# Two attention problems in one kernel: softmax reciprocals moved to GpSimd as powers, and the early loads and phi(K) exps placed anew

## The chip, the cores and the metric

The kernel runs on one core of one Trainium2 chip. The core has TensorE (PE, matrix products), VectorE (DVE), ScalarE (ACT), GpSimd (POOL) and SyncE (SP, which here only issues transfers). Each engine works through its own instructions in their order; semaphores tie them together. The metric is the device time of one execution in microseconds.

## The reference

Two attention blocks are computed side by side, and their outputs are concatenated. Each has sequence length 2048, width 512, 32 heads of 16 (`DH`). Problem B is plain softmax attention. Problem A is "infini-attention" in four segments of 512 tokens: causal softmax inside a segment, plus a read of a memory that the earlier segments filled. All inputs are bf16.

```python
# A, for each segment s of 4
phi = lambda t: jnp.where(t > 0, t + 1.0, jnp.exp(t))
p = _softmax(qs @ ks.T * scale + mask)          # causal inside the segment
a_dot = p @ vs
a_mem = (phi(qs) @ M) / (phi(qs) @ z + 1e-06)
o = g * a_mem + (1.0 - g) * a_dot               # g = sigmoid(beta), per head
M = M + phi(ks).T @ vs ;  z = z + phi(ks).sum()
# B
p = _softmax(q @ k.T * Dh ** (-0.5)) ;  o = p @ v
# both: o @ wo, then concatenate
```

The two divisions matter here: the softmax's by its row sum, and the memory read's by `phi(q) z + 1e-06`.

## The kernel before

**Tiling and order.** Work is cut into units. A unit is one problem, one chunk of 512 queries and one group of 8; a group `hg` holds 4 heads, one in each 32-row band of TensorE's array. There are 32 units of A (4 segments by 8 groups) and 32 of B. Six A units come first, then A and B units are mixed. Two neighbouring groups share a tile `rt` of Q and K (even and odd heads in one 32-row band, told apart by a mask on Q).

For each unit TensorE makes scores into PSUM. Most score blocks get their exp on ScalarE (lines 690, 693, 757). For B, up to 22 blocks of a unit get it on VectorE instead: line 809 turns a 128x512 block into the bits of a rough power of two, line 775 adds two offsets, and three products with scaled copies of V (`VD`, made on GpSimd at line 626) sum to the exp. In A, GpSimd then zeroes the masked part (line 704). TensorE accumulates the product with V into one PSUM bank `acc` (line 915). A column of ones in V gives the row sum as column 16 (`DH`).

**The planner.** Which instruction follows which is decided while the program is built. A loop keeps a clock for each engine (`c["t"]` for TensorE, `c["act"]`, `c["dve"]`, `c["gp"]`), charged by costs in ns (`dve_do`, `act_do`, `gp_do`). It chooses between a score tile, a product with V, and "chores" (projections, memory sums, output projections). A chore has a due time and may have a condition on the clock: `WA_AT` is the earliest planner time at which A's remaining V, K and Q weights may be used, `XB_AT` and `WB_AT` the same for B's transposed inputs and weights. `pick` moves blocks of a B unit from VectorE to ScalarE where the blocks left for VectorE (1050 ns each) would outlast those left for ScalarE (470 ns each). Small filler products with zeros (line 898) keep TensorE busy.

**Start.** Lines 74 to 78 load four tiles of A's X and the first 128 columns of `wk_a` (on ScalarE's queue) and `wq_a` (on SyncE's). TensorE transposes X (line 303), ScalarE and VectorE copy it (line 944), TensorE projects the first Q and K (lines 948, 949), VectorE masks Q (952, 955), and ScalarE copies K (953). The other transfers were issued early on SyncE: `wv_a`, the rest of `wk_a` and `wq_a` (167 to 169), B's transposed X in four parts (173) with B's weights after the first part (176), and the output weights (182, 183). Three memsets of VectorE (92, 93) write one column of each remaining A weight tile first, so that these three transfers wait for them.

**phi(K).** For each K tile of A, `phi_k` issues a transposing transfer on SyncE (line 390). Later, at a planner time 12000 ns past VectorE's clock, ScalarE takes the exp (394) and GpSimd makes min, max and sum (396 to 398). The memory sum `chore_macc` uses it.

**Ends of units.** `finalize` transposes `acc` into `tT` on VectorE (846), takes the reciprocal of column 16 into a slot of `RA` on VectorE (849), and GpSimd multiplies (863 for A's gate, 867 to 870). For the last unit VectorE multiplies. All of `RA` is tested for its range at the end. `chore_am`, the memory read of an A unit, transposes on VectorE (491), adds 1e-6 (494), takes the reciprocal (495), and GpSimd multiplies (498). Of these reads there are 24, of `finalize` 64.

Of the kernel before, what the change touches and what calls it, by code (L numbers as in the profile page):

```python
# [10 lines left out]
ALU = mybir.AluOpType  # L11
AX = mybir.AxisListType
F32 = mybir.dt.float32
F16 = mybir.dt.float16
BF16 = mybir.dt.bfloat16
# [4 lines left out]
P = 128  # L20
H = 32
DH = 16
D = H * DH
# [18 lines left out]
def fast_path(ctx, tc, nc, A_x, A_wq, A_wk, A_wv, A_wo, A_beta, B_x, B_wqkv, B_wo, out, flag):  # L42
# [19 lines left out]
    def wview(w):  # L62
        return w.rearrange("(cc p) n -> p cc n", p=P)
# [21 lines left out]
    n = 1  # L85
# [2 lines left out]
        n *= 2  # L88
    ri = const.tile([P, 32], F32, name="ri")
    nc.vector.transpose(ri[:], ci[:, 0:32])  # L90

    for w in (wv_a[:, 0, 0:1], wk_a[:, 0, P:P + 1], wq_a[:, 0, P:P + 1]):
        nc.vector.memset(w, 0.0)
    rb32 = const.tile([P, 1], F32, name="rb32")
    for j in range(4):
        nc.vector.memset(rb32[32 * j:32 * j + 32, :], 32.0 * j)
# [44 lines left out]
        nc.vector.memset(jm[32 * j:32 * j + 32, j:j + 1], 1.0)  # L141
    mqg = const.tile([P, 4, 2], F32, name="mqg")

    def setup_gates():

        nc.scalar.activation(gcol[:], beta_t[:], ACT.Exp, scale=-1.0)
        nc.vector.tensor_scalar(gcol[:], gcol[:], 1.0, None, ALU.add)
        nc.vector.reciprocal(gcol[:], gcol[:])
        nc.vector.tensor_scalar(omg[:], gcol[:], -1.0, 1.0, ALU.mult, ALU.add)
        g4, m4 = gcol[:].rearrange("p (r t) -> p r t", t=2), mq[:].unsqueeze(1).to_broadcast([P, 4, 2])  # L150
        nc.vector.tensor_tensor(mqg[:], g4, m4, op=ALU.mult)
        for par in range(2):
            to = maskg[:].rearrange("p (r t) j d -> p t r j d", t=2)[:, par]
            j4 = jm[:].unsqueeze(1)
            nc.gpsimd.tensor_tensor(to[:, :, :, DH], j4.to_broadcast([P, 4, 4]), mq[:, par:par + 1].unsqueeze(2).to_broadcast([P, 4, 4]), op=ALU.mult)
            for rt in range(4):
                nc.gpsimd.tensor_tensor(to[:, rt, :, 0:DH], jm[:].unsqueeze(2).to_broadcast([P, 4, DH]),
                                        mqg[:, rt, par:par + 1].unsqueeze(2).to_broadcast([P, 4, DH]), op=ALU.mult)
# [5 lines left out]
    nc.vector.tensor_scalar(sati[:], sat[:], EXP_B, 0.0, ALU.add, ALU.max)  # L164
    nc.vector.tensor_scalar(sat[:], sati[:], 32767.0, None, ALU.is_equal)

    nc.sync.dma_start(out=wv_a[:], in_=wview(A_wv))
    nc.sync.dma_start(out=wk_a[:, :, P:], in_=wview(A_wk)[:, :, P:])
    nc.sync.dma_start(out=wq_a[:, :, P:], in_=wview(A_wq)[:, :, P:])

    xT_b = const.tile([P, 4, S], BF16, name="xT_b")
    def load_xb(q):
        nc.sync.dma_start_transpose(out=xT_b[:, :, q * 512:(q + 1) * 512], in_=xb2[q * 512:(q + 1) * 512, :])
    load_xb(0)
    for w, part in ((wk_b[:], 1), (wq_b[:], 0), (wv_b, 2)):
        nc.sync.dma_start(out=w, in_=wview(B_wqkv)[:, :, part * D:(part + 1) * D])
    for q in range(1, 4):
        load_xb(q)

    WA_AT = dict(v=6000, k=7000, q=8200)  # L180
    XB_AT, WB_AT = (11000, 16000, 19500, 23000), dict(k=12500, q=13000, v=13500)
    nc.sync.dma_start(out=wo_a[:], in_=wview(A_wo))
    nc.sync.dma_start(out=wo_b[:], in_=wview(B_wo))


    E1 = [(9, 0), (10, 1), (11, 2), (13, 0), (14, 1), (15, 2)]
# [80 lines left out]
    def dve_do(ns, ready):  # L267
        c["dve"] = max(c["dve"], ready) + ns
        return c["dve"]
# [12 lines left out]
    def at(time, fn):  # L282
        lcount[0] += 1
        heapq.heappush(later, (time, lcount[0], fn))
# [102 lines left out]
    def phi_k(s, rt):  # L387

        kn = phik_t[(s, rt)] = sb_.tile([P, 4, P], BF16, name="phik", tag="xin", bufs=4)
        nc.sync.dma_start_transpose(out=kn[:], in_=KT_at[(s, rt)][:])  # L390

        def more():
            e = sb_.tile([P, 4, P], BF16, name="ek", tag="e", bufs=2)
            nc.scalar.activation(e[:], kn[:], ACT.Exp)
            act_do(act_cost(512) + 100, c["t"])
            nc.gpsimd.tensor_scalar(e[:], e[:], 1.0, 0.0, ALU.min, ALU.max)
            nc.gpsimd.tensor_scalar(kn[:], kn[:], 3e38, 0.0, ALU.min, ALU.max)
            nc.gpsimd.tensor_tensor(kn[:], kn[:], e[:], op=ALU.add)
            gp_do(1024, c["act"] + LAT)
            gp_do(512, 0, 2.1)  # L400
            phik_at[s] = c["gp"] + LAT
            phik_n[s] = phik_n.get(s, 0) + 1
        at(c["dve"] + 12000, more)

    def chore_k(k, s, rt):
        def evac(bank):
# [77 lines left out]
    def chore_am(u):  # L484
        def fill(bank, _):
            quad(bank, mbds[(u["c"] - 1) % 2][:, u["hg"], :, :].rearrange("p j w -> p (j w)"),
                 PHQ[(u["c"], u["rt"])][0][:], True, True)

        def evac(bank):
            aT = sb_.tile([P, 16, 32], F32, name="aT", tag="aT", bufs=1)  # L490
            nc.vector.transpose(aT[:].rearrange("p c d -> p (c d)"), bank)
            d_done(dve_do(dve_cost(512), c["t"] + LAT))
            r2 = sb_.tile([P, 16, 1], F32, name="r2", tag="r2", bufs=2)
            nc.vector.tensor_scalar(r2[:], aT[:, :, DH:DH + 1], 1e-6, None, ALU.add)
            nc.vector.reciprocal(r2[:], r2[:])  # L495
            dve_do(400, 0)
            tM = sb_.tile([P, 16, DH], F32, name="tM", tag="tM", bufs=2)
            nc.gpsimd.tensor_tensor(tM[:], aT[:, :, 0:DH], r2[:].to_broadcast([P, 16, DH]), op=ALU.mult)  # L498
            gp_do(256, c["dve"] + LAT, 2.1)
            aT_at[0] = c["gp"]  # L500
            u["am"] = tM
        d_job(fill, evac, False)
# [338 lines left out]
    def finalize(u, last):  # L841
        i, hg = u["i"], u["hg"]
        assert u["k"] == "b" or u["c"] == 0 or u["am"] is not None
        key = (u["k"], u["c"], u["rt"])
        tT = sb_.tile([P, 16, 32], F32, name="tT", tag="tT", bufs=2)
        nc.vector.transpose(tT[:].rearrange("p c d -> p (c d)"), u["acc"][:])  # L846
        acc_free[0] = dve_do(dve_cost(512), c["t"] + LAT)
        rr = RA[:, u["slot"], :].unsqueeze(2)
        nc.vector.reciprocal(rr, tT[:, :, DH:DH + 1])  # L849
        dve_do(170, 0)  # L850
        if u["par"] == 0:
            tN_t[key] = sb_.tile([P, 8, 32, 2], BF16, name="tN", tag="tN", bufs=3)
        dst = tN_t[key][:].rearrange("p c f t -> p c t f")[:, :, :, DH * u["par"]:DH * u["par"] + DH]
        src = tT[:].rearrange("p (t c) d -> p c t d", t=2)[:, :, :, 0:DH]
        eng = nc.vector if last else nc.gpsimd
        gp_do(256, c["dve"] + LAT, 2.1)
        if u["k"] == "a":
            gp_do(16, 0)
        if u["am"] is not None:
            gp_do(256, 0, 2.1)  # L860
        if u["k"] == "a":
            rw = sb_.tile([P, 16, 1], F32, name="rw", tag="rw", bufs=2)
            eng.tensor_scalar(rw[:], rr, omg[:, hg:hg + 1], 1.0, ALU.mult, ALU.mult)
            rr = rw[:]
        rb = rr.rearrange("p (t c) o -> p c t o", t=2).to_broadcast([P, 8, 2, DH])
        if u["am"] is None:
            eng.tensor_tensor(dst, src, rb, op=ALU.mult)  # L867
        else:
            eng.tensor_tensor(src, src, rb, op=ALU.mult)
            eng.tensor_tensor(dst, src, u["am"][:].rearrange("p (t c) d -> p c t d", t=2), op=ALU.add)  # L870
        if u["par"] == 1:
            def turn():
                OT = sb_.tile([P, 8, 32, 2], BF16, name="OT", tag=f"OT_{u['k']}", bufs=5)
                nc.vector.transpose(OT[:].rearrange("p c r t -> p (c r t)").bitcast(F32),
                                    tN_t[key][:].rearrange("p c f t -> p (c f t)").bitcast(F32))
                dve_do(dve_cost(256), 0)
                OT_t[key] = OT
                if u["rt"] == 3 and not last:
                    for sbl in range(4):
                        chore(0, lambda sbl=sbl: chore_out(u["k"], u["c"], sbl), due=prog[0] + 6000 + 4000 * sbl)  # L880
                    order_chores()
            if last:
                turn()
            else:
                at(max(c["dve"], c["gp"]) + 300, turn)
# [55 lines left out]
    for n in range(2):  # L941
        bank = d_bank(BF16)
        fill_xT(bank, (2 * n, 2 * n + 1))
        (nc.scalar.copy if n == 0 else nc.vector.tensor_copy)(
            xt0.rearrange("p c (i s) -> p i c s", s=P)[:, 2 * n:2 * n + 2], bank.rearrange("p (n c s) -> p n c s", n=2, c=4))
    (_, pq), (_, pk) = s_tile(), s_tile()
    warm_up(2)
    proj(pq[:, 0, :], range(4), wq_a[:], rsl(0), xt0)
# [1 line left out]
    qt0 = sb_.tile([P, 2, 512], BF16, name="QT_a", tag="QT_a", bufs=QTB["a"])  # L950
    QT_at[(0, 0)] = qt0
    nc.vector.tensor_scalar(qt0[:, 0, :], pq[:, 0, :], mq[:, 0:1], None, ALU.mult)
    nc.scalar.copy(k_dst("a", 0, 0), pk[:, 0, :])
    k_ready[("a", 0, 0)] = 0.0
    nc.vector.tensor_scalar(qt0[:, 1, :], pq[:, 0, :], mq[:, 1:2], None, ALU.mult)
# [661 lines left out]
```

## Time and profile before

| what | value |
|---|---|
| median of 3 runs (lowest to highest) | 907.6 us (907.23 to 915.0) |
| profiled execution | 912.13 us, its span 910.4 us |
| granted TensorE clock, mean | 0.966 |
| transfers over the span | 15.79 MB |
| score tiles exp'd on ScalarE, line 757 | 595 of 128x1536 or less, mean 1249 ns |
| score blocks exp'd on VectorE, line 809 | 588 of 128x512, mean 674 ns |
| causal select on GpSimd, line 704 | 192, mean 524 ns |

The profile is of one execution, and times in it are from the span's start. "Busy" is the time in which an engine executes. The chain of waits is followed back from the last instruction: at each step to what released it, or to the instruction before it on its engine. In a row of a group, the first figures are busy time in us and the mean of one instruction in ns; after the bar stands the engine's idle time just before them, and what ended it. PEld is TensorE's loading of weights, SPq and ACTq the issuing part of SyncE and ScalarE. The granted clock is a share of full speed.

### The profile page before, as it was taken

How to read it: one execution, taken by the hardware profiler on the slowest of the kernel's cores; microseconds unless marked ns; L12 is line 12 of the kernel's file. 1: busy time of each engine (PE TensorE's matmuls, PEld its weight loads, DVE VectorE, ACT ScalarE, POOL GpSimd, SP SyncE). 2: the span in 40 equal slices, each digit the busy share in tenths (PEclk: the TensorE clock that was granted, in tenths of full speed). 3: DMA queues.
4: the chain of work that ended last, by engine and by line, in shares of the span. 5: the costliest groups of instructions: out<-in, count | busy, mean ns of one | idle time of the engine just before them, and what ended most of it. 6: DMA issues, size and time to landing. Idle time of an engine off the chain costs nothing.

```text
span 910.4 us, 23979 instructions
## 1 busy us (share of the span) xinstructions
PE 794.5 (87%) x9915; PEld 268.7 (30%) x9915; DVE 789.9 (87%) x1606; ACT 839.9 (92%) x785; POOL 390.8 (43%) x779
## 2 busy tenths in 40 slices
PE   7898889988888888998888988888989988888796
PEld 3232223323233222332222323232322222223232
DVE  3457878898999989979999989998899899999985
ACT  5699979989999999999999999898999999999994
POOL 4853325354253155533541554425443333454330
PEclk9999979999999999999999999899999999999997
DMA  8700100000000010010000000100000000000000
GB/s 190 130 2 1 30 2 13 19 8 2 1 8 19 7 31 2 1 25 8 8 1 13 19 2 7 26 1 1 25 2 1 25 1 1 2 2 1 2 25 28
DMA packets 31800, 15.79 MB, mean 17 GB/s; under 512 B 22977, under 2 KB 31681, under 8 KB 31681
## 3 DMA queue, kind: packets, MB, share of 16 engines
q1 hardware_dynamic: 30448, 13.51, 6.8%
q8 instruction: 79, 1.29, 0.6%
q10 hardware_dynamic: 1104, 0.66, 0.2%
q14 instruction: 41, 0.33, 0.1%
q0 software_dynamic: 128, 0.00, 0.0%
HBM read 4.72 MB, written 4.19 MB: 10 GB/s over the span
## 4 chain that ended last, share of the span: by engine, by line
ACT 30%; PE 27%; DVE 26%; issue 11%; POOL 4%; DMA 1%; ACTq 0%; SPq 0%; DVEq 0%
ACT pT L757 26%; DVE pD L809 11%; DVE pD L775 9%; PE acc L915 9%; PE d_ps L325 6%; PE s_ps L752 5%; ACT pT L693 3%; DVE tT L846 2%; PE s_ps L683 2%; PE d_ps L798 2%; PE acc L898 1%; POOL pT L704 1%; DMA wq_a<-in_A_wq_dram 1%; POOL VD L626 1%; DVE RA L849 1%
## 5 line engine op out<-in xcount | busy, mean ns | idle before, releaser
L757 ACT ACTIVATE pT<-s_ps 128x1536 bf16<-128x1536 f32 (+1 forms) x595 | 674.5, 1249 | 33.1 <-PE d_ps L798 21.0
L809 DVE TENSOR_SCALAR pD<-d_ps 128x512 int16<-128x512 f32 x588 | 380.8, 674 | 29.0 <-PE d_ps L798 25.8
L752 PE MATMUL s_ps<-QT_b,KT_b 32*128 32x512 bf16 x1460 | 237.1, 393 | 58.9 <-ACT pT L757 52.6
L775 DVE TENSOR_SCALAR pD<-pD 128x1024 int16<-128x1024 int16 (+1 forms) x612 | 266.1, 477 | 0.7
L915 PE MATMUL acc<-pD,VD 128*32 128x512 f16 x1764 | 226.2, 397 | 6.4 <-DVE tT L846 5.5
L915 PE MATMUL acc<-pT,VP_b 128*32 128x512 bf16 x1460 | 230.8, 394 | 0.0
L798 PE MATMUL d_ps<-QT_b,KT_b 32*128 32x512 bf16 x588 | 212.1, 389 | 17.7 <-DVE pD L809 13.5
L704 POOL TENSOR_SCALAR_AFFINE_SELECT pT<-pT 128x512 bf16<-128x512 bf16 (+3 forms) x192 | 96.7, 524 | 203.2 <-ACT pT L693 201.6
L693 ACT ACTIVATE pT<-s_ps 128x1024 bf16<-128x1024 f32 (+1 forms) x128 | 137.9, 1147 | 12.7 <-PE s_ps L683 10.8
L752 PEld LDWEIGHTS <-KT_b 32*128 32x128 bf16 x1460 | 71.1, 91 | 259.3 <-issue 249.3
L898 PE MATMUL acc<-ident,zero 128*32 128x256 bf16 (+1 forms) x1400 | 84.2, 300 | 2.0 <-DVE tT L846 1.7
L915 PEld LDWEIGHTS <-VD 128*32 128x32 bf16 x1764 | 62.8, 97 | 74.1 <-issue 56.0
L626 POOL TENSOR_SCALAR VD<-VP_b 128x288 bf16<-128x288 bf16 x192 | 73.5, 383 | 21.5 <-DVE VP_b L450 8.0
L915 PEld LDWEIGHTS <-VP_b 128*32 128x32 bf16 x1460 | 62.5, 97 | 51.8 <-issue 35.0
L683 PE MATMUL s_ps<-QT_a,KT_a 32*128 32x384 bf16 (+3 forms) x512 | 56.3, 302 | 12.0 <-ACT pT L693 7.2
L846 DVE STREAM_TRANSPOSE tT<-acc 128x512 f32<-128x512 f32 x64 | 45.2, 706 | 21.9 <-PE acc L915 19.8
L898 PEld LDWEIGHTS <-zero 128*32 128x32 bf16 x1404 | 32.6, 96 | 70.6 <-issue 67.1
L798 PEld LDWEIGHTS <-KT_b 32*128 32x128 bf16 x588 | 46.9, 91 | 16.0 <-issue 13.8
L498 POOL TENSOR_TENSOR tM<-aT,r 128x256 f32<-128x256 f32 x24 | 16.0, 665 | 62.9 <-DVE r L495 62.6
L867 POOL TENSOR_TENSOR tN<-tT,RA 128x256 bf16<-128x256 f32 x31 | 20.2, 651 | 45.0 <-DVE RA L849 44.9
L915 PE MATMUL acc<-pT,VP_a 128*32 128x384 bf16 (+3 forms) x512 | 36.8, 312 | 2.3 <-POOL pT L704 2.0
L683 PEld LDWEIGHTS <-KT_a 32*128 32x128 bf16 x512 | 18.6, 91 | 67.6 <-issue 62.2
(114 smaller groups left out, 633.1 us busy)
## 6 DMA issues: line engine op xcount, KB each, us to landing
out_dram<-osb SPq DMA_DIRECT2D x30, 128.0 KB, 1.7
wv_a<-in_A_wv_dram SPq DMA_DIRECT2D x1, 512.0 KB, 10.9
wk_b<-in_B_wqkv_dram SPq DMA_DIRECT2D x1, 512.0 KB, 4.9
wq_b<-in_B_wqkv_dram SPq DMA_DIRECT2D x1, 512.0 KB, 5.8
wv_b<-in_B_wqkv_dram SPq DMA_DIRECT2D x1, 512.0 KB, 6.7
wo_a<-in_A_wo_dram SPq DMA_DIRECT2D x1, 512.0 KB, 4.7
wo_b<-in_B_wo_dram SPq DMA_DIRECT2D x1, 512.0 KB, 5.5
wk_a<-in_A_wk_dram SPq DMA_DIRECT2D x1, 384.0 KB, 11.6
```

Of the source, the lines that this page charges most:

```text
L626: mul = lambda dst, src: nc.gpsimd.tensor_scalar(dst, src, EXP_C[k], 1.0, ALU.mult, ALU.mult)
L683: nc.tensor.matmul(pt[:, b, col:col + w], kt[32 * j:32 * j + 32, kbl * P:(kbl + 1) * P], q[32 * j:32 * j + 32, P * kbl:512], start=(r == 0 ...
L693: nc.scalar.activation(pT[:].rearrange("p b n -> p (b n)")[:, 0:n], pt[:].rearrange("p b n -> p (b n)")[:, 0:n], ACT.Exp, scale=0.25)
L704: nc.gpsimd.affine_select(out=blk, in_=blk, compare_op=ALU.is_ge, fill=0.0, base=0, pattern=[[0, e - b], [0, w // P], [1, P]], channel_mul ...
L752: nc.tensor.matmul(pt[:, b, :], KT_b[32 * j:32 * j + 32, u["rt"], kb * P:(kb + 1) * P], q[32 * j:32 * j + 32, :], start=True, stop=True, t ...
L757: nc.scalar.activation(pT[:, 0:n, :], pt[:, 0:n, :], ACT.Exp, scale=1.0 / (LOG2E * 1024.0))
L775: nc.vector.tensor_scalar(tile[:, k, 0:n, :], tile[:, 0, 0:n, :], EXP_D[k], None, ALU.add)
L798: nc.tensor.matmul(bank, KT_b[32 * j:32 * j + 32, u["rt"], kb * P:(kb + 1) * P], qslice(u)[32 * j:32 * j + 32, :], start=True, stop=True, ...
L809: nc.vector.tensor_scalar(pd[:, 0, n, :], bank, EXP_B, 0.0, ALU.add, ALU.max)
L846: nc.vector.transpose(tT[:].rearrange("p c d -> p (c d)"), u["acc"][:])
L898: nc.tensor.matmul(bank[32 * j:32 * j + 32, 0:w].rearrange("p (n q) -> p n q", q=P), zero[:, 0:32], ident[:].unsqueeze(1).to_broadcast([P, ...
L915: nc.tensor.matmul(u["acc"][32 * j:32 * j + 32, e["c0"]:512], e["lhsT"], e["rhs"], start=(j not in u["started"]), stop=False, tile_positio ...
```

## The change

Four things are changed.

1. The reciprocals at 849 (except for the last unit) and 495 become a `tensor_tensor` on GpSimd with the operation `pow` and a tile `neg1` of -1. The addition of 1e-6 at 494 becomes a `tensor_scalar` on GpSimd. The planner charges GpSimd 100 + 16 x 20 = 420 ns for each of these instructions, and no longer charges VectorE 170 or 400.
2. A's remaining weights are issued by ScalarE right after its copy of X (`load_rest_a`). The three memsets that they waited for go.
3. B's inputs and the output weights are issued by SyncE later (`load_b`): a memset of VectorE behind the first masked Q writes into `xT_b`, and the first transfer waits for it. Their order becomes x(0), wk, wv, x(1), wq, x(2), x(3), `wo_a`, `wo_b`; before it was x(0), wk, wq, wv, x(1) to x(3), `wo_a`, `wo_b`.
4. The planner's earliest times follow: `WA_AT`, `XB_AT` and `WB_AT` as below, and the exps of phi(K) come no earlier than `PHI_AT` = 31000.

```diff
-    for w in (wv_a[:, 0, 0:1], wk_a[:, 0, P:P + 1], wq_a[:, 0, P:P + 1]):
-        nc.vector.memset(w, 0.0)
...
+    neg1 = const.tile([P, 16], F32, name="neg1")
+    nc.gpsimd.memset(neg1[:], -1.0)
...
-    WA_AT = dict(v=6000, k=7000, q=8200)
-    XB_AT, WB_AT = (11000, 16000, 19500, 23000), dict(k=12500, q=13000, v=13500)
...
+    def load_rest_a():
+
+        nc.scalar.dma_start(out=wv_a[:], in_=wview(A_wv))
+        nc.scalar.dma_start(out=wk_a[:, :, P:], in_=wview(A_wk)[:, :, P:])
+        nc.scalar.dma_start(out=wq_a[:, :, P:], in_=wview(A_wq)[:, :, P:])
+
+    def load_b():
+
+        def x(q):
+            nc.sync.dma_start_transpose(out=xT_b[:, :, q * 512:(q + 1) * 512], in_=xb2[q * 512:(q + 1) * 512, :])
+
+        def w(t, part):
+            nc.sync.dma_start(out=t, in_=wview(B_wqkv)[:, :, part * D:(part + 1) * D])
+        nc.vector.memset(xT_b[:, 0, 0:1], 0.0)
+        x(0)
+        w(wk_b[:], 1)
+        w(wv_b, 2)
+        x(1)
+        w(wq_b[:], 0)
+        x(2)
+        x(3)
+        nc.sync.dma_start(out=wo_a[:], in_=wview(A_wo))
+        nc.sync.dma_start(out=wo_b[:], in_=wview(B_wo))
+
+    WA_AT = dict(v=6500, k=8500, q=10000)
+    XB_AT, WB_AT = (10000, 18000, 23500, 28000), dict(k=13500, v=16000, q=21000)
+    PHI_AT = 31000
...
-        at(c["dve"] + 12000, more)
+        at(max(c["dve"] + 12000, PHI_AT), more)
...
-            nc.vector.tensor_scalar(r2[:], aT[:, :, DH:DH + 1], 1e-6, None, ALU.add)
-            nc.vector.reciprocal(r2[:], r2[:])
-            dve_do(400, 0)
+            nc.gpsimd.tensor_scalar(r2[:], aT[:, :, DH:DH + 1], 1.0, 1e-6, ALU.mult, ALU.add)
+            nc.gpsimd.tensor_tensor(r2[:], r2[:], neg1[:].unsqueeze(2), op=ALU.pow)
+            gp_do(16, c["dve"] + LAT, 20.0)
+            gp_do(16, 0)
...
-        nc.vector.reciprocal(rr, tT[:, :, DH:DH + 1])
-        dve_do(170, 0)
+        if last:
+            nc.vector.reciprocal(rr, tT[:, :, DH:DH + 1])
+        else:
+            nc.gpsimd.tensor_tensor(rr, tT[:, :, DH:DH + 1], neg1[:].unsqueeze(2), op=ALU.pow)
+            gp_do(16, c["dve"] + LAT, 20.0)
...
+        if n == 0:
+            load_rest_a()
...
+    load_b()
```

More of the change, by code (lines that the diff above doesn't have):

```diff
@@ L165, in fast_path @@
     nc.vector.tensor_scalar(sat[:], sati[:], 32767.0, None, ALU.is_equal)
-    nc.sync.dma_start(out=wv_a[:], in_=wview(A_wv))
-    nc.sync.dma_start(out=wk_a[:, :, P:], in_=wview(A_wk)[:, :, P:])
-    nc.sync.dma_start(out=wq_a[:, :, P:], in_=wview(A_wq)[:, :, P:])
     xT_b = const.tile([P, 4, S], BF16, name="xT_b")
[L172 to L178, printed above, removed]
-    WA_AT = dict(v=6000, k=7000, q=8200)
-    XB_AT, WB_AT = (11000, 16000, 19500, 23000), dict(k=12500, q=13000, v=13500)
-    nc.sync.dma_start(out=wo_a[:], in_=wview(A_wo))
-    nc.sync.dma_start(out=wo_b[:], in_=wview(B_wo))
+    def load_rest_a():
[20 more added lines that the diff above has]
+    PHI_AT = 31000
     E1 = [(9, 0), (10, 1), (11, 2), (13, 0), (14, 1), (15, 2)]
```

## The prediction

> **What bounds the kernel now.** The profiled execution took 912.1 us (span 910.4); the median of the runs shown is 907.6, so 4.5 less. I read the busy shares first, then the chain of waits.
>
> ```profile
> PE 794.5 (87%) x9915; PEld 268.7 (30%) x9915; DVE 789.9 (87%) x1606; ACT 839.9 (92%) x785; POOL 390.8 (43%) x779
> ...
> ACT 30%; PE 27%; DVE 26%; issue 11%; POOL 4%; DMA 1%; ACTq 0%; SPq 0%; DVEq 0%
> ```
>
> No engine owns the chain: ScalarE, TensorE and VectorE share it about equally, GpSimd has 4% (some 36 us). A saving on one of them is therefore worth a fraction of itself in the long middle. The table of stages shows where that is not so (columns: stretch, its length, busy time and instructions of PE, weight loads, DVE, ACT, POOL, granted clock, DMA share, GB/s):
>
> ```profile
> 0.00:13.50 13.50, 8.64 (x60) 3.65 (x60) 5.08 (x32) 2.88 (x3) 6.64 (x32) 0.87 0.69 151
> 13.50:30.00 16.50, 15.09 (x252) 5.87 (x251) 8.35 (x17) 12.22 (x14) 11.74 (x29) 1.00 1.08 222
> 30.00:45.00 15.00, 11.93 (x165) 4.30 (x165) 6.24 (x10) 10.05 (x13) 11.66 (x23) 0.89 0.57 105
> 45.00:60.00 15.00, 15.00 (x236) 6.52 (x228) 9.39 (x18) 13.82 (x15) 12.11 (x23) 1.00 0.01 3
> 60.00:880.00 820.00, 722.67 (x8959) 240.32 (x8952) 740.15 (x1490) 783.55 (x728) 340.32 (x670) 0.97 0.04 9
> ```
>
> From 60 to 880 us ScalarE is 96% and VectorE 90% busy. In the first 60 us ScalarE is idle for 21 us, of which the first 10.6 are the start. The chain in that stretch, in order of time (start, length, what), names two transfers:
>
> ```profile
> 1.70 7.46 DMA wq_a<-in_A_wq_dram
> 9.16 0.04 issue
> 9.21 3.21 PE s_ps L325 x32
> ...
> 27.34 2.54 ACT pT L693 x3
> 29.88 5.54 DMA phik<-KT_a
> ```
>
> First, TensorE waits for A's first query weights until 9.21, 2.8 us by the list of waits. Second, an exp of ScalarE waits for a transposed K. The timeline shows it (start, length, engine, line; SPq is SyncE's issuing):
>
> ```profile
> 4.27 11.42 SPq L173 DMA_TRANSPOSE xT_b<-in_B_x_dram  x1
> ...
> 17.46 11.14 SPq L173 DMA_TRANSPOSE xT_b<-in_B_x_dram  x3
> ...
> 28.64 0.59 SPq L182 DMA_DIRECT2D wo_a<-in_A_wo_dram  x1
> ...
> 29.28 0.51 SPq L183 DMA_DIRECT2D wo_b<-in_B_wo_dram  x1
> ...
> 35.45 0.63 ACT L394 ACTIVATE ek<-phik 128x512 bf16<-128x512 bf16 x1 [3.41 <-DMA phik<-KT_a]
> ```
>
> K's transpose stands behind all of B's loads and is issued only at 29.88. The exp, put early into ScalarE's order, blocks every later exp for 3.41 us. TensorE stands still from 34 to 37 us and comes back at half clock: the windows give 0.50 from 37 to 40. The same follows the wait at the start (idle 6.5 to 9.2, then 0.50 from 10 to 12.5).
>
> **What the Trainium skill says.** "TensorE: Matmul & The Clock Gate", Part 1: the array falls to half clock after about 3.4 us of idleness, and needs about 3.4 us of work to rise again. The two stretches agree in kind, after only 2.7 and 3.0 us of idleness. "DMA: Bandwidth & Descriptors", Issuing engines are not separate DMA queues: transfers of every issuing queue run on the same 16 engines and interleave, so ScalarE's queue alone gives A's weights no bandwidth. The trace can only hint: the moved rate falls from 280 to 303 GB/s (2 to 4 us) to 145 to 178 (7 to 11 us) after the first B transpose is issued at 4.27. "GPSIMD Engine Reference", section 3.1: two-input elementwise work costs some 2.6 cycles per element plus dispatch; the page has no figure for a power. Section 8 there: GpSimd shares SBUF interfaces with VectorE; no run here isolates that.
>
> **Part 1: A's other weights and the gate on B.** Removed: three VectorE memsets (0.06 us each). SyncE loses three issues (0.37, 0.51, 0.43 us); ScalarE gets them after its xT copy (end 5.72). That is 1.3 us of ScalarE, covered by its 6.72 us wait ahead of the K cast at 12.44 (still over 2 us of cover if that cast comes 4 us sooner). B's loads wait for one VectorE memset (0.06) behind the first masked Q. So until both first weight tiles land only X, the two 128 KB tiles and beta compete. Without the wait TensorE could start when xT is complete, at 6.25: 2.8 us sooner, with clock still up. Its 32 matmuls then take about 2.1 instead of 3.21 us (16 take 1.05 in the full-clock rows): 1.1 more. V's projections may start 500 planner ns later than before, so I take off 0.5: **3.4 us**. Ends: 0 (the 256-byte pieces are slow in themselves; at 5 to 6 us the DMA engines are nearly idle at 14 GB/s, which speaks for that), or a loss of 1 if A's remaining weights, now asked for 3 us later, are late for TensorE.
>
> **Part 2: B's loads and phi(K).** On SyncE x(0) now starts near 8 us. Issuing it took 11.42 us behind A's weights, the other three 11.14/3 = 3.7 each; weights take 1.6 and the two output weights 1.2. So phik's issue moves from 29.88 to between 8+3.7+1.6+11.1+1.2 = 25.6 and 33.3, landing 5.5 later: 31.1 to 38.8. The planner's clock runs 9.1 us behind the trace now (V due at 6000, first V matmul at 15.13), about 5.7 after part 1; PHI_AT of 31000 puts the exps near 36.7. Mostly the data is there: 3.41 us of idleness go, plus 1.1 of the idleness at half clock behind it; TensorE's full 45 to 60 stage may give 1 back. **3.5 us**; ends 1 (late transfers: 2.1 left, or B's later-due projections missing as filling) and 5. Later phi(K) itself costs nothing: its first consumer, the memory sum, is evicted at 129.4 us. Its three GpSimd operations (0.61+0.61+1.16) may bunch with the causal selects; that is in the lower end.
>
> **Part 3: the reciprocals.** The rows (shape, count, busy us, mean ns):
>
> ```profile
> L849 DVE RECIPROCAL RA<-tT 128x16 f32<-128x16 f32 x64 | 16.2, 253 | 2.2
> ...
> L863 POOL TENSOR_SCALAR rw<-RA,omg 128x16 f32<-128x16 f32 x32 | 10.2, 320 | 9.0 <-DVE RA L849 8.4
> ...
> L494 DVE TENSOR_SCALAR r<-aT 128x16 f32<-128x16 f32 x24 | 7.4, 309 | 0.8
> ...
> L495 DVE RECIPROCAL r<-r 128x16 f32<-128x16 f32 x24 | 6.1, 253 | 0.8
> ```
>
> VectorE loses 63 x 0.253 + 24 x 0.309 + 24 x 0.253 = 29.4 us. The planner frees less, 63 x 170 + 24 x 400 ns = 20.3 us, and hands VectorE about 20.3/(1.05+0.47) = 13 more score blocks. Each takes 0.42 us (1249/3) from ScalarE and costs VectorE 0.674 + 266.1/588 = 1.13, TensorE some 0.2. So ScalarE -5.5, VectorE -14.7, TensorE +2.6. Weighted by their chain shares over their busy time (273/840, 237/790, 246/795): -1.8, -4.4, +0.8: about **-5.5 us**. Ends: 0 and -9.
>
> GpSimd gains 24 sums at L863's 0.32 (7.7 us) and 87 powers, which no trace here shows. Floor: 0.32, the nearest shape. The planner charges 0.42; I take it: 36.5 us. Together +44 on 391 busy, at 36/391 up to +4.1 us of chain. The page's waits put only 2.0 us of TensorE on GpSimd's selects, and its wait for the reciprocal goes as well, so I take half: **+2 us**, ends 0 and +4 at this price. neg1's memset (about 0.1) falls in GpSimd's empty stretch from 7.5 to 17.1: nothing.
>
> Sum: -3.4 - 3.5 - 5.5 + 2 = -10.4; 912.1 becomes 901.7 as a profiled execution, and the median of 907.6 becomes **897**.
>
> **Rivals.** (a) Slower, by one mechanism: the power is long on GpSimd. The finalize and memory powers stand ahead of causal selects, Q masks and VD pieces on its in-order queue, and TensorE waits for those in its own order. By the share of the chain each microsecond of price adds 87 x 36/391 = 8.0 us. The other parts gain 12.4, the sums cost 0.7: break-even at a price of 1.5 us, slower by over 1% from 2.6. At 3 us: 907.6 - 12.4 + 0.7 + 24 = 920. For it: a power is no simple operation and no row prices it. Against: 16 elements per partition, and GpSimd is 57% idle. Chance 0.18.
> (b) The transfers only trade places: the first weights land as before, or B's transposes, issued while A's weights still move, make TensorE wait at V, K or Q. Parts 1 and 2 give together 0 to 2: 907.6 - 1 - 3.5 = 903. For it: the nearly idle DMA engines at 5 to 6 us. Against: the whole front waits on named transfers. Chance 0.17.
> (c) The order comes out as reckoned: 897, own range 888 to 904. Chance 0.65.
>
> **How the numbers follow.** A measurement of this kernel tells about 1% (9 us) from no change: the bounds are 898.5 and 916.7. Case (c) straddles the lower one: 0.50 faster, 0.15 the same. (b): 0.02, 0.14, 0.01. (a): 0, 0.03, 0.15. So 0.52 faster, 0.32 the same, 0.16 slower. The range 885 to 915 leaves out most of (a)'s slower part (0.15) and little below.
>
> **What would show it.** First projection near 6.3 us at clock 1.0, first exp near 9.5; no wait of L394 for DMA; the reciprocals on VectorE fall to 2 (the gates' and the last), score blocks there rise from 588 to about 601; GpSimd's power row near 0.4 us; its select still holds TensorE for only a few us. Wrong if the power's row exceeds 1 us, if TensorE waits for wv_a, wk_a or xT_b, or if the ScalarE idleness in the first 60 us stays near 21 us.

## The result, and the profile after

The changed kernel takes 1046.45 us (median of 4 runs, 1043.09 to 1051.79) against 907.41 for the kernel before: ratio 1.1515, 95% interval 1.1435 to 1.1594. It is 139 us slower, where 897 was forecast. In the ratios here and below, runs more than 1.5% above the fastest of the same kernel are left out as slow: three of e11's 22, and two of the 59 of the kernel before beside it. The profiled execution took 1044.7 us (span 1043.0), close to the median.

From the page of the changed kernel: the engines' busy time, the chain of waits by engine, and three groups (busy us, mean ns of one | idle time before, and what ended it). Line numbers have shifted: 849 is now 865, 495 is 507, 704 is 717.

```profile
PE 847.1 (81%) x9921; PEld 276.7 (27%) x9921; DVE 772.2 (74%) x1502; ACT 846.2 (81%) x785; POOL 648.4 (62%) x891
...
POOL 31%; PE 25%; ACT 22%; DVE 10%; issue 10%; DMA 1%; ACTq 0%; DVEq 0%; POOLq 0%
...
L865 POOL TENSOR_TENSOR RA<-tT,neg 128x16 f32<-128x16 f32 x63 | 187.2, 2972 | 38.7 <-DVE tT L859 38.3
...
L931 PE MATMUL acc<-pT,VP_a 128*32 128x384 bf16 (+3 forms) x512 | 55.8, 341 | 79.8 <-POOL pT L717 79.1
...
L507 POOL TENSOR_TENSOR r<-r,neg 128x16 f32<-128x16 f32 x24 | 70.7, 2946 | 2.0
```

The row of that product before the change, in the page of the kernel before:

```profile
L915 PE MATMUL acc<-pT,VP_a 128*32 128x384 bf16 (+3 forms) x512 | 36.8, 312 | 2.3 <-POOL pT L704 2.0
```

A power of 16 columns takes 2.97 us on GpSimd; the reciprocal on VectorE took 0.253. GpSimd's busy time rises from 391 to 648 us, and the two rows of powers make 258 us. It is still idle for 38% of the span, yet its share of the chain goes from 4 to 31%. TensorE's wait for the causal select (line 717) rises from 2.0 to 79.1 us.

The timeline of the changed kernel shows one such delay (start, length, engine, line, what):

```profile
32.56 2.92 POOL L865 TENSOR_TENSOR RA<-tT,neg 128x16 f32<-128x16 f32 x1
...
35.57 0.28 POOL L879 TENSOR_SCALAR rw<-RA,omg 128x16 f32<-128x16 f32 x1
35.94 0.64 POOL L883 TENSOR_TENSOR tN<-tT,rw 128x256 bf16<-128x256 f32 x1
36.53 2.75 POOL L717 TENSOR_SCALAR_AFFINE_SELECT pT<-pT 128x512 bf16<-128x512 bf16 x6
...
37.46 0.37 PE L931 MATMUL acc<-pT,VP_a 128*32 128x256 bf16 x1 [3.24 <-POOL pT L717]
...
38.82 0.61 PE L696 MATMUL s_ps<-QT_a,KT_a 32*128 32x128 bf16 x5
...
39.53 1.24 ACT L706 ACTIVATE pT<-s_ps 128x1280 bf16<-128x1280 f32 x1 [4.19 <-PE s_ps L696]
...
55.66 0.63 ACT L406 ACTIVATE ek<-phik 128x512 bf16<-128x512 bf16 x1 [6.35 <-POOL phik L410]
```

Read it downwards. The power holds GpSimd until 35.48. The unit's multiplications follow, and only then six selects, which run without a gap. TensorE, in its own order, stands 3.24 us before a product with V that needs one of them; behind it stand the next scores; and ScalarE, which has nothing to do with the reciprocal, is idle for 4.19 us. The last line is the other thing to notice. The phi(K) exp no longer waits for its transfer, but it does wait, for GpSimd.

The table of stages of the changed kernel (length; busy time of PE, PEld, DVE, ACT, POOL; granted clock, DMA share, GB/s):

```profile
13.50:30.00 16.50, 14.95 (x238) 5.79 (x234) 8.22 (x16) 11.92 (x15) 12.74 (x27) 1.00 1.10 219
30.00:45.00 15.00, 10.84 (x118) 3.25 (x110) 4.13 (x7) 7.37 (x9) 14.64 (x20) 0.77 0.54 104
45.00:60.00 15.00, 9.33 (x122) 3.47 (x120) 4.68 (x8) 7.80 (x10) 14.16 (x22) 0.81 0.01 2
```

In the last two of these stages GpSimd is the full engine (14.64 and 14.16 of 15 us), and ScalarE falls to half (10.05 and 13.82 us before). TensorE is busy less, and its granted clock is lower: 0.77 and 0.81, against 0.89 and 1.00. That holds over the span as well: 0.902 in the mean, 0.966 before.

### The profile page after: what moved, and what is told of

Read it like the earlier page. It is cut to its first block, busy times and chain, and to the rows that moved or that the text cites. A ratio compares the mean times of both kernels' runs of the same rounds, so it can differ in the third digit from the quotient of the medians.

```text
span 1043.0 us, 23982 instructions
## 1 busy us (share of the span) xinstructions
PE 847.1 (81%) x9921; PEld 276.7 (27%) x9921; DVE 772.2 (74%) x1502; ACT 846.2 (81%) x785; POOL 648.4 (62%) x891
## 3 DMA queue, kind: packets, MB, share of 16 engines
HBM read 4.72 MB, written 4.19 MB: 9 GB/s over the span
## 4 chain that ended last, share of the span: by engine, by line
POOL 31%; PE 25%; ACT 22%; DVE 10%; issue 10%; DMA 1%; ACTq 0%; DVEq 0%; POOLq 0%
ACT pT L770 18%; POOL RA L865 10%; PE acc L931 9%; POOL pT L717 6%; PE s_ps L765 6%; PE d_ps L337 5%; DVE pD L822 5%; DVE pD L788 4%; ACT pT L706 4%; POOL r L507 3%; POOL VD L639 2%; PE d_ps L811 2%; PE acc L914 2%; POOL tN L883 2%; POOL QT_a L356 1%
## 5 line engine op out<-in xcount | busy, mean ns | idle before, releaser
L770 ACT ACTIVATE pT<-s_ps 128x1536 bf16<-128x1536 f32 (+2 forms) x595 | 678.2, 1236 | 148.3 <-PE d_ps L811 94.6
L765 PE MATMUL s_ps<-QT_b,KT_b 32*128 32x512 bf16 x1455 | 249.4, 412 | 52.1 <-ACT pT L770 46.5
L931 PE MATMUL acc<-pD,VD 128*32 128x512 f16 x1779 | 240.1, 417 | 2.7 <-DVE pD L788 1.6
L865 POOL TENSOR_TENSOR RA<-tT,neg 128x16 f32<-128x16 f32 x63 | 187.2, 2972 | 38.7 <-DVE tT L859 38.3
L765 PEld LDWEIGHTS <-KT_b 32*128 32x128 bf16 x1455 | 69.3, 92 | 268.1 <-issue 258.4
L931 PE MATMUL acc<-pT,VP_a 128*32 128x384 bf16 (+3 forms) x512 | 55.8, 341 | 79.8 <-POOL pT L717 79.1
L507 POOL TENSOR_TENSOR r<-r,neg 128x16 f32<-128x16 f32 x24 | 70.7, 2946 | 2.0
L696 PE MATMUL s_ps<-QT_a,KT_a 32*128 32x512 bf16 (+3 forms) x512 | 57.2, 306 | 13.6 <-ACT pT L706 7.0
L356 POOL TENSOR_SCALAR QT_b<-qc,mq 128x512 bf16<-128x512 bf16 x32 | 24.0, 761 | 52.8 <-DVE qc L448 52.6
L890 DVE STREAM_TRANSPOSE OT<-tN 128x256 f32<-128x256 f32 x32 | 14.2, 443 | 52.2 <-POOL tN L883 36.7
```

The costliest lines, as they stand in the source:

```text
L507: nc.gpsimd.tensor_tensor(r2[:], r2[:], neg1[:].unsqueeze(2), op=ALU.pow)
L765: nc.tensor.matmul(pt[:, b, :], KT_b[32 * j:32 * j + 32, u["rt"], kb * P:(kb + 1) * P], q[32 * j:32 * j + 32, :], start=True, stop=True, t ...
L770: nc.scalar.activation(pT[:, 0:n, :], pt[:, 0:n, :], ACT.Exp, scale=1.0 / (LOG2E * 1024.0))
L865: nc.gpsimd.tensor_tensor(rr, tT[:, :, DH:DH + 1], neg1[:].unsqueeze(2), op=ALU.pow)
L931: nc.tensor.matmul(u["acc"][32 * j:32 * j + 32, e["c0"]:512], e["lhsT"], e["rhs"], start=(j not in u["started"]), stop=False, tile_positio ...
```

## The experiments

All ratios are to the kernel before, measured beside the run. The median is over all runs. Two runs stand outside the table: e7 (one run, 922.9 us) and e12 (the kernel before once more, 911.1 us).

| run | reciprocals | charge to GpSimd | loads | median us | ratio (95% interval) |
|---|---|---|---|---|---|
| changed kernel | power | 420 ns | new | 1046.45 | 1.1515 (1.1435 to 1.1594) |
| e1 | VectorE | none | new | 910.12 | 1.001 (0.9989 to 1.0031) |
| e2 | power | 420 | old | 1046.9 | 1.1534 (1.1483 to 1.1585) |
| e3 | power | 2916 | new | 969.05 | 1.0666 (1.0625 to 1.0708) |
| e4 | cheap stand-in | 420 | new | 906.56 | 0.998 (0.996 to 0.9999) |
| e5 | power at unit ends only (63) | 420 | new | 1030.21 | 1.133 (1.1271 to 1.1389) |
| e6 | power in memory reads only (24) | 420 | new | 953.92 | 1.0485 (1.0423 to 1.0548) |
| e10 | cheap stand-in | 2916 | new | 927.99 | 1.0205 (1.0152 to 1.0259) |
| e8 | VectorE, phi exps spaced | none | new | 907.87 | 0.9978 (0.9956 to 1.0) |
| e9 | as e8, V weights sooner | none | new, changed | 905.96 | 0.9962 (0.9941 to 0.9983) |
| e11 | VectorE, phi exps spaced | none | old | 907.31 | 0.995 (0.9924 to 0.9976) |

**e1 and e2: which half of the change.** e1 puts both reciprocals back and keeps the rest; e2 does the reverse.

```diff
# e1, against the changed kernel
+            nc.vector.tensor_scalar(r2[:], aT[:, :, DH:DH + 1], 1e-6, None, ALU.add)
+            nc.vector.reciprocal(r2[:], r2[:])
+            dve_do(400, 0)
...
+        nc.vector.reciprocal(rr, tT[:, :, DH:DH + 1])
+        dve_do(170, 0)
# e2, against the kernel before: the changed lines of these two places, and neg1
```

> The changed kernel with both reciprocals (and the addition of 1e-6) back on VectorE and charged there as before; the loads, their planner times and the later phi(K) exps stay. If the loss is all the power's, this is part 1 and part 2 of the prediction alone: 907.4 - 7 = about 900 us, no wait of the phi(K) exp for its transfer. If the transfers only trade places: 904 to 907. If the new order of loads is itself part of the loss: over 912.

> The kernel before with the reciprocals as powers on GpSimd (and the 1e-6 there), nothing else. If the power's price is the whole loss: 1046 + 5 = about 1051 us, within 1040 to 1060. If the two parts hurt each other (B's later loads behind a late GpSimd): clearly below 1030.

e2 is as slow as the whole change, so the loss comes with the powers. e1 shows that the new loads and the later phi(K) in sum neither cost nor gain (1.001); at 910 us it fits none of the three ranges given. That is the second surprise, taken up below.

**e4: the place without the price.** The power becomes a multiplication by 1e-9, at the same place, with the same operands and charge.

```diff
-    nc.gpsimd.memset(neg1[:], -1.0)
+    nc.gpsimd.memset(neg1[:], 1e-9)
...
-            nc.gpsimd.tensor_tensor(rr, tT[:, :, DH:DH + 1], neg1[:].unsqueeze(2), op=ALU.pow)
+            nc.gpsimd.tensor_tensor(rr, tT[:, :, DH:DH + 1], neg1[:].unsqueeze(2), op=ALU.mult)
```

> The changed kernel with a multiplication by a constant of 1e-9 in place of each power: same operands, places, waits and charges; the reciprocal is left out. If only the power's duration is to blame: one of these takes about 0.3 us, and the time is what the prediction summed, 890 to 905 us. If moving the step to GpSimd at all (its queue, the hop between engines) costs: over 930.

The rows of the score blocks on VectorE and of the stand-in, in e4's groups:

```profile
L822 DVE TENSOR_SCALAR pD<-d_ps 128x512 int16<-128x512 f32 x593 | 387.0, 677 | 34.7 <-PE d_ps L811 30.2
...
L865 POOL TENSOR_TENSOR RA<-tT,neg 128x16 f32<-128x16 f32 x63 | 16.2, 257 | 45.4 <-DVE tT L859 45.1
```

With the cheap operation at 0.257 us the kernel takes 906.6 us, just over the expected 890 to 905, as e1's loads bring nothing. Against e1, measured beside it, it gains 3.6 us. Moving the step to another engine is harmless by itself; without the power's duration there is no loss. (Leaving the reciprocal out changes the values that are passed on, but the granted clock of e4's runs, 0.969 to 0.984, is within that of e1's, 0.967 to 0.986.)

**e3 and e10: the plan or the engine.** The planner counted 0.42 us for a power. In e3 it counts what the trace shows. e10 is that plan with the cheap stand-in (the reciprocal left out).

```diff
-            gp_do(16, c["dve"] + LAT, 20.0)
-            gp_do(16, 0)
+            gp_do(16, c["dve"] + LAT, 8.0)
+            gp_do(16, 0, 176.0)
...
-            gp_do(16, c["dve"] + LAT, 20.0)
+            gp_do(16, c["dve"] + LAT, 176.0)
```

> The changed kernel, but the planner charges GpSimd what the trace shows: 2916 ns for a power (0.42 before), 228 ns for the addition. If the loss comes from a plan made with a wrong price (TensorE ordered to wait for selects that GpSimd has not reached): under 970 us, and TensorE's wait for the causal select falls from 79 us to under 25. If GpSimd's 258 us of powers cost of themselves, in whatever order: over 1010.

> The kernel with the charge of 2916 ns, but with the multiplication by 1e-9 in place of each power (the reciprocal is left out). If what remained there (969 against 907 with a cheap operation and a small charge) is GpSimd's real time: 905 to 920. If it is the plan itself, which spaces the work for a slow GpSimd: 945 to 969.

The four kernels with two prices and two charges make a square, in ratios: 0.998 (cheap, low charge), 1.0205 (cheap, high), 1.0666 (power, high), 1.1515 (power, low). Against the cheap pair, the power costs 0.1535. Of that, 0.0849 (77 us of 907), more than half, vanishes when the plan knows the price. Of the rest, 0.0461 (42 us) is what the slow instruction costs in a plan that knows it, and 0.0225 (20 us) is that plan itself, which costs this even with a cheap operation. The split follows this one path through the square: the order made at the low price costs nothing while the operation is cheap (0.998), so the 77 us belong to the duration and the wrong order together. Both theories hold a part: e3, at 969 us, came just under the 970 given for the plan, and e10, at 928, fell between its two ranges.

From the list of waits, first the changed kernel, then e3 (us in total, times, longest):

```profile
PE acc L931 <- POOL pT L717: 79.1, 54, 5.3
```

```profile
PE acc L931 <- POOL pT L717: 24.4, 34, 2.3
```

With the true charge TensorE still waits for selects, but never more than 2.3 us at a time. The mean granted clock of e3's runs is 0.964 to 0.978, that of the changed kernel's 0.894 to 0.907. e3's plan also holds some 500 more of the small filler products with zeros (1896 against 1400); no run separates what they, the clock and the order of the other work each give.

**e5 and e6: which powers.** Each keeps one of the two places on GpSimd, at the low charge.

> The changed kernel with the memory sum's addition and reciprocal back on VectorE; the 63 powers at the ends of units stay on GpSimd, charged 420 ns. If each power costs alike: 910 + 63/87 x 137 = about 1009 us. If the memory's 24 are the worse ones, because TensorE waits for the accumulation behind them: under 990.

> The changed kernel with the reciprocals at the ends of units back on VectorE; the 24 powers of the memory read stay on GpSimd, charged 420 ns. If each power costs alike: 910 + 24/87 x 137 = about 948 us. If GpSimd's empty time takes up a few long instructions (loss only above some load): under 925.

Over e1's 910.1 the 63 cost 120 us and the 24 cost 44: 1.9 and 1.8 us each, so a power costs about the same in both places. But 120 + 44 = 164 is more than the 136 of both together. The losses overlap, and e5 and e6 lie 21 and 6 us above the proportional guesses. Even 24 powers are not taken up by GpSimd's idle half.

**e7: what a power costs.** Added to the kernel before, in GpSimd's early order:

```diff
+    for w in (1, 4, 16, 64):
+        nc.gpsimd.tensor_tensor(pb[:, 128:128 + w], pb[:, 0:w], pb[:, 64:64 + w], op=ALU.pow)
+    nc.gpsimd.tensor_tensor(pb[:, 192:208], pb[:, 0:16], pb[:, 64:80], op=ALU.mult)
```

> The kernel before with six added groups of instructions on GpSimd in its empty stretch at the start: two memsets, powers of 128x1, 128x4, 128x16 and 128x64 f32 with an exponent tile of -1, one multiplication of 128x16. If a power's 2.9 us is a cost for each element: about 0.3, 0.8, 2.9 and over 10 us. If it is a cost for each instruction: all four near 2.9 us. The multiplication near 0.25 us.

The groups of e7, shapes kept apart (line 147 holds the powers, 148 the product):

```profile
L147 POOL TENSOR_TENSOR RA<-RA 128x64 f32<-128x64 f32 x1 | 10.5, 10547 | 0.1
...
L147 POOL TENSOR_TENSOR RA<-RA 128x16 f32<-128x16 f32 x1 | 2.9, 2900 | 0.1
...
L147 POOL TENSOR_TENSOR RA<-RA 128x4 f32<-128x4 f32 x1 | 1.0, 1025 | 0.1
L147 POOL TENSOR_TENSOR RA<-RA 128x1 f32<-128x1 f32 x1 | 0.6, 588 | 9.5 <-issue 9.5
...
L148 POOL TENSOR_TENSOR RA<-RA 128x16 f32<-128x16 f32 x1 | 0.2, 218 | 0.0
```

From 16 to 64 columns the time rises by 7.65 us, or 159 ns for each column; from 1 to 16 by 154. So a power costs some 0.43 us plus 0.16 us a column. The planner had 20 ns a column, eight times too little. (e7 itself took 922.9 us in its one run: GpSimd's added work, with the powers from 17.2 to 32.5 us, holds up the first selects, for which TensorE waits 17.0 us.)

**e8, e9, e11, e12: where the gain of the loads went.** e1's own trace names two new waits. From its timeline:

```profile
10.72 3.28 ACT L702 ACTIVATE pT<-s_ps 128x1280 bf16<-128x1280 f32 x3 [0.55 <-PE s_ps L692]
...
14.24 1.05 PE L334 MATMUL d_ps<-wv_a,xT_a 128*32 128x512 bf16 x8 [1.40 <-DMA wv_a<-in_A_wv_dram]
...
15.87 1.02 ACT L702 ACTIVATE pT<-s_ps 128x1024 bf16<-128x1024 f32 x1 [1.87 <-PE s_ps L692]
...
47.82 0.63 ACT L403 ACTIVATE ek<-phik 128x512 bf16<-128x512 bf16 x1 [3.11 <-POOL phik L407]
```

From its table of stages (columns as before; the granted clock is the third figure from the end):

```profile
13.00:14.00 1.00, 0.00 (x0) 0.00 (x0) 0.00 (x0) 1.00 (x1) 0.00 (x0) 0.57 1.60 189
...
19.00:20.00 1.00, 1.00 (x9) 0.15 (x9) 0.69 (x1) 0.46 (x1) 1.00 (x3) 0.51 1.08 375
```

ScalarE starts at 10.72 instead of 13.52. Then TensorE waits for A's V weights until 14.24, and its clock is about half from 13 to 20 us. By 60 us ScalarE has been busy for 38.68 us, against 38.97 in the kernel before: the gain is gone. Later, PHI_AT lets several exps come due together; the third wants a scratch tile of two buffers that GpSimd's phi sum still holds. The 3.41 us wait for a transfer has become a 3.11 us wait for GpSimd. e8 spaces the exps; e9 also issues `wv_a` behind the first part of `wk_a`; e11 spaces them in the kernel before.

```diff
# e8 and e9, against the changed kernel (and the reciprocals back on VectorE, as in e1)
-        at(max(c["dve"] + 12000, PHI_AT), more)
+        at(max(c["dve"] + 12000, PHI_AT + (3500 * rt if s == 0 else 0)), more)
# e9 also
+    nc.scalar.dma_start(out=wv_a[:], in_=wview(A_wv))
...
-        nc.scalar.dma_start(out=wv_a[:], in_=wview(A_wv))
# e11, against the kernel before
-        at(c["dve"] + 12000, more)
+        at(max(c["dve"] + 12000, 29000 + 3500 * rt if s == 0 else 0), more)
```

> The kernel with the new loads and the reciprocals on VectorE, and phi(K)'s exps of segment 0 set 3500 planner ns apart (31000, 34500, 38000, 41500) instead of together. If ScalarE's 3.1 us wait for GpSimd's phi sum (the scratch tile of two buffers, with three exps at once) is what gave back the gain of part 2: that wait goes, 904 to 907 us. If the stretch before 60 us is held by TensorE anyway: 909 to 911.

> The same, and A's V weights issued on ScalarE's queue right behind the first 128 columns of K's, some 2.5 us sooner. If the late V weights and TensorE's half clock behind them gave back the gain of part 1: no wait for them, 901 to 905 us. If the first weights then land late again, as in the kernel before: no better than without it, 904 to 911.

> The kernel before, with phi(K)'s exps of segment 0 no earlier than planner times 29000, 32500, 36000 and 39500; nothing else. If the 3.41 us wait for the transfer, and TensorE's half clock behind it, bounded the early stage: 903 to 905 us. If other work is late next: 906 to 909.

In all three no phi(K) exp waits in the first 60 us. e9 has no wait for V weights either (e8 has one of 3.2 us). e9 and e11 gain 0.4 and 0.5% with intervals clear of 1, so they are faster than the kernel before, by little; e8's interval ends at 1.0. The medians of all of e11's runs and of the kernel before (907.31 and 910.04) give 0.3%. e8 and e9 came out 1 us above the ranges given for a cure, e11 within the second of its two; the kernel before stood at 910.0 beside them, so the ratios decide. These differences of 2 to 4 us are small against the spread of the kernel before, whose runs beside these three went from 902.7 to 918.2. With the exps spaced in both, the new loads (e8, 907.9) bring nothing over the old (e11, 907.3); what is gained goes with the spacing, and some 2 us more in e9 with the earlier V weights, both barely clear of the noise.

e12 is the kernel before, profiled again.

> The kernel before, unchanged, profiled a second time. If its start is a property of the kernel: first exp of ScalarE near 13.5 us again, the first query weights landing 7.5 us after their issue, and the phi(K) exp waiting some 3.4 us for its transfer. If the landing was a draw of that one execution: first exp between 9.5 and 11 us, as in the two other kernels with the same loads, and the wait for the transfer as long or longer, since ScalarE then reaches that exp sooner.

Its timeline (span 909.4, against 910.4 of the first profile):

```profile
14.92 3.28 ACT L693 ACTIVATE pT<-s_ps 128x1280 bf16<-128x1280 f32 x3 [0.71 <-PE s_ps L683]
...
40.04 0.63 ACT L394 ACTIVATE ek<-phik 128x512 bf16<-128x512 bf16 x1 [5.39 <-DMA phik<-KT_a]
```

Whether the late start is a draw or belongs to this program stays open. With the old loads, the first exp came at 13.52 and 14.92 us in the kernel before, and at 10.56 (e2), 9.82 (e7) and 10.55 us (e11) in the three others; with the new ones (the changed kernel, e1, e3 to e6, e8, e10) at 9.17 to 11.87, half of them before 9.7. e12 went the way of its first branch and beyond the values given there: it began later than ever. And although ScalarE was busy 5 us less in the first 60 us than in the first profile (33.97 against 38.97), the span is 1 us shorter. From 100 to 880 us ScalarE was busy for 749.60 us, against 743.55 in the first profile: two executions of one kernel differ there by some 6 us, nearly what parts 1 and 2 together were to bring.

## Why the prediction was wrong, point by point

**The failed step is the price in part 3**: "The planner charges 0.42; I take it: 36.5 us." It measured 2.96, so 258 us. The prediction had written that no trace shows a power, and that only the floor (0.32) was known. It then took as its value a number from the program under test, which is an assumption of the code and not a measurement. The program's wrong number did harm twice: it entered the forecast, and it made a plan that, with these powers in it, is 77 us slower than e3's. For that second effect the prediction put nothing, and gave no reason.

**The rival's slope failed too.** It named the mechanism, the queue and the place correctly: "ahead of causal selects". But "each microsecond of price adds 87 x 36/391 = 8.0 us" would give some 20 us for the 2.54 us above 0.42, so that even the right price would have summed to about 920. Against e4's stand-in, 2.7 us shorter, the loss was 140 us, or 52 per microsecond. In plans that know the price, e3 against e10, the same 2.7 us cost 41 us, or 15 per microsecond. So most of the miss lies in the plan. That fits its arithmetic: a power runs 2.5 us past what the planner counted, ten times the 0.25 us that it leaves between a producer and its consumer. The rest is that a share of the chain is no steady slope: GpSimd's was 4% before, 10% in e4 with 30 us more of work, 1% in e10, and 31% in the changed kernel. Break-even at 1.5 us rested on that slope and on a gain of 12.4 us that did not come; where it lies was not tried.

**Part 3 without the price came out right in sum**: -5.5 for VectorE and +2 for GpSimd, together -3.5; e4 against e1 gives -3.6. That close an agreement is partly luck, for the terms were not right one by one: VectorE's score blocks rose from 588 to 593, not 601, and GpSimd's share of the chain rose to 10%. The reciprocals left VectorE as said.

**Part 1 (-3.4) and part 2 (-3.5) were right in their waits and wrong in their sum**: e1 gives +0.1% (interval -0.1 to +0.3%). For part 1, the first query weights did land sooner (3.4 to 5.9 us after their issue in nine profiles with the new loads, 4.7 to 8.2 in five with the old), but the forecast rested on one execution, in which they landed 2 to 3 us later than in the three other kernels with the same loads. A's remaining V weights were asked for at 4.70 us in the changed kernel, before the first weights had landed, and not behind ScalarE's copy at 5.72 as reckoned. The forecast's own lower end, "A's remaining weights [...] are late for TensorE", then came true: in six of eight profiles (all with the new loads but e9's) TensorE waits 1.2 to 3.2 us for `wv_a`, and e1's ScalarE idleness in the first 60 us is 21.3 us, as the prediction's signs of being wrong had it. For part 2, the wait for the transfer went as reckoned. Bunched GpSimd work was named, but as a matter of the causal selects and not of the exps' own scratch tile, and its price was not worked out. e11, with spaced exps and old loads, gains 0.3 to 0.5% (2.7 to 4.5 us), which is of the size that part 2 had claimed.

**The clock** agrees with the Trainium skill, "TensorE: Matmul & The Clock Gate" (Part 1), in kind only. The page gives half clock after an idle window of about 3.4 us, and full clock after about 3.4 us of sustained work. In e1 half clock comes within the wait of 1.40 us for the V weights, after four microseconds in which TensorE was 45 to 83% busy, and holds for nearly 6 us of work (14.24 to 20 us); these measured lengths, and not the page's, are what this kernel pays. No run separates the clock from the waits that cause it.

## What to carry to other kernels

Price an instruction that no trace shows by a probe of its own or keep a wide range: the planner's constant, the engine's idle share and the element count are no price. An engine that is half idle but feeds others in order had no room here for instructions of 3 us; what counts is how long one instruction holds up the queue against the slack of the consumers behind it, and whether the plan knows that length. When a wait is removed in a staged start, list what is asked for next and which small buffer it shares, and look at more than one execution before counting a wait for a transfer.

## What the runs showed of the hardware that was not expected

A power on GpSimd costs about 0.43 us plus 0.16 us for each column of 128 partitions (588, 1025, 2900 and 10547 ns for 1, 4, 16 and 64), where a product of 16 columns takes 218 ns. VectorE's reciprocal of 16 columns takes 253. The landing of the first 128 KB of query weights, issued at 1.7 us, took 4.7, 4.7, 5.3, 7.5 and 8.2 us in five executions of four kernels with the same loads.
